# Two tiles' turns moved from TensorE to the DMA, and epsilon of two tiles moved to VectorE

## The chip, the core and the metric

The kernel runs on one core of one Trainium2 chip. The metric is the device time of one execution in microseconds (us). The kernel before takes 200.3 us, the median of three runs (200.17 to 200.72).

## What is computed

A parallel block: an attention branch A and a gated MLP branch B read the same normalised input, and both results are added to it.

```python
def _A_ref(x, wqkv, wo):            # 32 heads of 16; 8 keys, 2 apart, behind each query
    qkv = (x @ wqkv) ...
    logits = jnp.einsum('bhsd,bhswd->bhsw', q, kg) * scale
    attn = _softmax(where(mask, logits, -1e9))
    o = jnp.einsum('bhsw,bhswd->bhsd', attn, vg)
    return o.transpose(...) @ wo
def _B_ref(x, w_in, w_sp, b_sp, w_out):
    z = _gelu(x @ w_in)
    z1, z2 = z[..., :Fh], _layernorm(z[..., Fh:])
    g = jnp.einsum('ts,bsf->btf', w_sp, z2) + b_sp[None, :, None]
    return (z1 * g) @ w_out
xn = _layernorm(x)
return x + _A_ref(xn, A_wqkv, A_wo) + _B_ref(xn, B_w_in, B_w_sp, B_b_sp, B_w_out)
```

There are 2048 rows of x with 512 columns; Fh is 688. All inputs are bf16.

## The kernel before

The rows of x are 16 tiles of 128. Every step of the work is a named operation (`op_`, line 153) with a list of the operations it needs. Five lists at the end (lines 594 to 640), one for each of TensorE (`pe`), ScalarE (`act`), VectorE (`dve`), GpSimd (`pool`) and the SP queue (`sp`), fix by hand the order in which each engine runs its operations. So the order of an engine never changes at run time: an operation that waits holds up all that stand behind it in its list.

The names, in the order of the work (i is a tile):

- `x{i}` loads x, `b{i}` and `ag{i}` (lines 172 to 176) make mean and variance on VectorE, `gr{i}` (line 178) makes 1/sqrt(variance + epsilon) on GpSimd in two instructions, an add of epsilon (L179) and a power (L180), and `n{i}` normalises on VectorE (L183). Tile 0 is normalised in two halves, `n0a` and `n0` (L187).
- The normalised tile is turned, rows to columns, into `xnT`. Tiles 0 to 7 (`NPE = 8`) are turned by TensorE: `T{i}` (L216), four 128x128 blocks into PSUM, and `Tc{i}` (L219), a copy on ScalarE. Tiles 8 to 15 are turned by DMA from the SP queue: `t{i}` (L199).
- `z{i}` and `y{i}` (L234) are 8 matmuls each, the right and left half of x @ w_in. Their gelus are on ScalarE: `h{i}` (L251) and `yg{i}` (L314). The left half's result z1 lies over x and the normalised tiles in SBUF, so that y{i} may come only after certain norms.
- The right half z2 is normalised: statistics (`zt`, `sq`, `zs`), roots on GpSimd (`zr0`, `zr4`, `zr8`, `zr12`), the scaling on VectorE for tiles 0 to 7 and on ScalarE for 8 to 15 (`zn{i}`, L305).
- `k0`..`k7`, `q0`..`q7`, `v0`..`v7` (L325) are 32 matmuls each; ScalarE copies them out (`kc`, `qc`, `vc`, L338). `kh0a`, `kh0b`, `kh1` to `kh3` and `vh` (L343, L344) are small DMAs that copy halos of k and v between partitions.
- Products of q and k on VectorE, `m{c}{th}` (L363; the first is `m00`), folded by accumulating DMAs that GpSimd issues, `f{c}{th}` (L371), and summed into the logits, `p{c}{th}` (L376 to L379). Then the softmax of each half of the rows: `X`, `e`, `u`, `i`, `C`. `e` and `i` are on ScalarE (L420, L411 and L412), `u` (L406 to L408) on VectorE. `a0.*`, `a1.*` (L430, L434, L443) multiply with v and add. `HW` is a small memset on VectorE behind `p31`, which frees the third buffer of w_sp.
- `M0` to `M15` (L479) mix z2 with w_sp, 32 matmuls each; `W0` to `W7` load w_sp turned, each for two M. ScalarE empties M{j} as `G{j}` (L495), VectorE multiplies with z1, `g{j}` (L497), and SP turns the result, `U{j}` (L484).
- At the end both branches' output products are summed in PSUM (`gf`, `ao`: L533, L540, L544), x is added (`E`, `F`), and the rows are stored.

`psum("mm", ...)` (line 204) hands out three PSUM tiles in turn: a z, y, k, q, v or M may start only when the reader of the one three places ahead of it in the TensorE list is done. `psum("aux", ...)` has two tiles for the turns.

The lists around the change, as they are before:

```python
pe  = wu T0a T0 B wd z0a T1 z0b T2 z1 T3 z2 T4 z3 T5 z4 T6 z5 T7 z6 z7 y0 y1 z8 z9 ... z14  k0 k1 q0 q1 k2 k3 ...
sp  = x0 x1 x2 x3 x4 x5 x6 x8 wy x12 wk wq wv t8 t9 ... t15 W0 kh0a kh0b W1 kh1 vh W2 W3 LO0 LO1 W4 U0 ...
dve = b0 ag0 b1 ag1 n0a n0 b2 ag2 n1 b3 n2 ...  zn4 .. zn7 m00 f00 p00 m01 zs8 m10 ... p31 HW u0 X1 C0 g0 a0.0 u1 ...
act = ... EL e0 G0 i0 G1 e1 i1 G2 G3 ...
```

Of the kernel before, what the change touches and what calls it, by code (L numbers as in the profile page):

```python
# [10 lines left out]
ALU = mybir.AluOpType  # L11
# [5 lines left out]
NT = S // P  # L17
# [15 lines left out]
EPS = 1e-5  # L33
# [9 lines left out]
def kernel(  # L43
# [19 lines left out]
    x2 = A_x.rearrange("b s d -> (b s) d")  # L63
# [11 lines left out]
    mv = sb.tile([P, NT, 2], F32, name="mv")  # L75
    rstd = sb.tile([P, NT], F32, name="rstd")
# [33 lines left out]
    z2 = z2_r[:].rearrange("p (i f) -> p i f", i=NT)  # L110
# [42 lines left out]
    def op_(name, after, f):  # L153
        assert name not in do, name
        do[name], needs[name] = f, list(after)

    def tok(i):
        return f"Tc{i}" if i < NPE else f"t{i}"

    NPE = 8  # L160
    ALLX = [tok(i) for i in range(NT)]
    ALLN = [f"n{i}" for i in range(NT)]

# [8 lines left out]
    def bn(i):  # L172
        V.bn_stats(stats[:, i, :], xs[:, i, :])  # L173

    def ag(i):
        V.bn_aggr(mv[:, i, :], stats[:, i, :])

    def root(i, n):
        G.tensor_scalar(rstd[:, i:i + n], mv[:, i:i + n, 1], EPS, 1.0, ALU.add, ALU.mult)  # L179
        G.tensor_tensor(rstd[:, i:i + n], rstd[:, i:i + n], mhalf[:, 0:n], ALU.pow)  # L180

    def norm(eng, i):
        eng.tensor_scalar(xn[i % 8], xs[:, i, :], mv[:, i, 0:1], rstd[:, i:i + 1], ALU.subtract, ALU.mult)  # L183

    def norm_half(n):
        c = slice(n * D // 2, (n + 1) * D // 2)
        V.tensor_scalar(xn[0][:, c], xs[:, 0, c], mv[:, 0, 0:1], rstd[:, 0:1], ALU.subtract, ALU.mult)  # L187

    for i in range(NT):
        op_(f"b{i}", [f"x{LX[i]}"], lambda i=i: bn(i))  # L190
        op_(f"ag{i}", [f"b{i}"], lambda i=i: ag(i))
        op_(f"gr{i}", [f"ag{i}"], lambda i=i: root(i, 1))
        if i == 0:
            op_("n0a", ["gr0"], lambda: norm_half(0))
            op_("n0", ["n0a"], lambda: norm_half(1))
        else:
            op_(f"n{i}", [f"gr{i}"] + ([tok(i - 8)] if i >= 8 else []), lambda i=i: norm(V, i))
        if i >= NPE:
            op_(f"t{i}", [f"n{i}"], lambda i=i: SP.dma_start_transpose(xnT[:, :, i * P:(i + 1) * P], xn[i % 8]))  # L199
# [111 lines left out]
    def make_y(i):  # L311
        over = [f"n{j}" for j in range(i * FP // D, (i * FP + FH - 1) // D + 1)] if i < 8 else ALLN + ALLX
        t = psum("mm", f"y{i}", f"yg{i}", [tok(i)] + over + ["wy"], lambda t: z_part(t, i, 0))
        op_(f"yg{i}", [f"y{i}"], lambda: A.activation(  # L314
            z1u[:, i, 0:FH].rearrange("p (a b) -> p a b", a=2), t[:, :, 0:FHALF], ACT.Gelu_apprx_tanh))


# [63 lines left out]
    for c, th in BUF:  # L381
        n = f"{c}{th}"
# [147 lines left out]
    def gated_full(i, start, stop, c=slice(0, D)):  # L530
        th, t0 = i // 8, (i % 8) * P
        for m in range(MF):
            PE.matmul(po[i][:, c], uT[th][:, m, t0:t0 + P], wout[:, m, c], start=(start and m == 0), stop=(stop and m == MF - 1))  # L533

    def attention_out(n, start, stop):
        th, s = n // 2, n % 2
        for r in range(2):
            for g in range(4):
                p = slice(32 * g, 32 * g + RN[r])
                PE.matmul(po[groups[n][g]], rest[th][r][p, s * P:(s + 1) * P], wrest[r][p, :],  # L540
                          start=(start and r == 0), stop=False, tile_position=(32 * g, 0))
        for d in range(DH):
            for g in range(4):
                PE.matmul(po[groups[n][g]], op[32 * g:32 * g + 32, th, d, s * P:(s + 1) * P], wo_r[32 * g:32 * g + 32, d, :],  # L544
                          start=False, stop=(d == DH - 1 and (stop or groups[n][g] == groups[3][3])), tile_position=(32 * g, 0))

    U = [[f"U{j}" for j in range(8 * th, 8 * th + 8)] for th in range(2)]
    EVM = [f"G{j}" for j in range(NT)] + ["Bc", "Tc4"]
    for n in (0, 1):
        op_(f"gf{n}", LO + U[0] + EVM, lambda n=n: [gated_full(i, True, False) for i in groups[n]])  # L550
        op_(f"ao{n}", [f"gf{n}", "a0.11"] + [f"V0{g}" for g in range(4)], lambda n=n: attention_out(n, False, True))
# [37 lines left out]
    for n, (t, c) in enumerate(pieces):  # L589
# [1 line left out]
        op_(f"Sl{n}", [f"Fl{n}"], lambda n=n, c=c: (SP, A, SP)[n].dma_start(out2[il * P:(il + 1) * P, c], o_of(il)[:, c]))  # L591


    pe = """wu T0a T0 B wd z0a T1 z0b T2 z1 T3 z2 T4 z3 T5 z4 T6 z5 T7 z6 z7 y0 y1 z8 z9 z10 z11 z12 z13 z14
        k0 k1 q0 q1 k2 k3 q2 q3 k4 k5 q4 q5 k6 k7 q6 q7
        v0 v1 v2 v3 v4 v5 v6 v7 z15 y2 y3 y4 y5 y6 y7 y8 y9 y10 y11 y12 y13 y14 y15
        M0 M1 M2 M3 M4 M5 M6 M7 M8 M9 M10 M11 M12 M13 M14 M15
        gf0 gf1 ao0 ao1 gf2 ao2 ao3""".split() + [f"gf3.{i}" for i in tail] + ["gfl0", "gfl1", "gfl2"]
    for n in pe:
        a, x = n[0], n[1:]  # L600
        if n in do:
            continue
        if n == "T0a":
            make_T0()
        elif a == "T":
            make_T(int(x))
        elif n == "z0a":
            make_z0()
        elif a == "z":
            make_z(int(x))  # L610
        elif a == "y":
            make_y(int(x))
        elif a in "qkv":
            make_heads(a, int(x))
# [79 lines left out]
```

## Time and profile before

| | us |
|---|---|
| median of three runs | 200.3 |
| the profiled execution's own time | 200.27 |
| its span in the profile | 198.5 |
| TensorE busy in the span | 194.2 |
| VectorE busy | 178.4 |
| ScalarE busy | 89.4 |
| GpSimd busy | 49.3 |

The span leaves out 1.77 us of the execution's own time that lie around it. In the profile PE is TensorE, PEld its weight loads, DVE is VectorE, ACT is ScalarE, POOL is GpSimd; SP has no row of busy time, since it only issues DMAs, and SPq, ACTq rows are issues. L234 is line 234. A row of a timeline gives the start, the duration, the engine, the line, the operation, the tile that is written and those that are read, the count, and in brackets the idle time ahead of it with what ended it. In the chain the work that ended last is followed back; its rows give the start and the length of a piece. "DMA to landing" is the time from the issue until the data has arrived. Different source tiles have one name in some rows: z stands for z1 and z2 and what lies over them, qk for the two halves of q and k.

### The profile page before, as it was taken

The page shows a single profiled execution, that of the slowest core. Times are in us where ns is not written, and L with a number is a line of the kernel's source. Part 1 is how long each engine was busy: PE and PEld are TensorE (multiplying, and loading weights), DVE is VectorE, ACT ScalarE, POOL GpSimd, SP SyncE. Part 2 cuts the span into 40 slices and gives each one's busy share as a digit, 9 for nine tenths or more (in the row PEclk, how much of TensorE's full clock was granted, in tenths as well). Part 3 has the DMA queues.
Part 4 walks back from the last instruction along what each step waited for, and adds up shares of the span by engine and source line. Part 5 has one row for each costly group of instructions (what it writes and reads, how often), then busy time and mean ns, then how long its engine had stood idle before and what let it go on. Part 6 is the DMA issues. An engine that isn't in the chain of part 4 may idle for free.

```text
span 198.5 us, 4606 instructions
## 1 busy us (share of the span) xinstructions
PE 194.2 (98%) x1957; PEld 122.0 (61%) x1960; DVE 178.4 (90%) x205; ACT 89.4 (45%) x130; POOL 49.3 (25%) x83
## 2 busy tenths in 40 slices
PE   8999999999999999999999999999999999999993
PEld 2566666666666666666666666666666654444442
DVE  4899896999979999988999999999999999997244
ACT  2587797875559885991462311111222110044000
POOL 5567222005992249363000000010111000000000
PEclk9999999999999999999999999999999999999999
DMA  5999566860979999998299999999999969204233
GB/s 156 355 363 212 102 135 137 96 131 6 182 141 173 204 168 179 169 181 162 48 229 229 165 220 236 193 181 225 262 185 109 242 116 259 45 3 147 68 106 106
DMA packets 69076, 32.87 MB, mean 166 GB/s; under 512 B 57312, under 2 KB 67072, under 8 KB 68928
## 3 DMA queue, kind: packets, MB, share of 16 engines
q1 hardware_dynamic: 65680, 24.15, 58.2%
q0 software_dynamic: 2688, 7.70, 21.2%
q10 hardware_dynamic: 688, 0.74, 1.3%
q8 instruction: 15, 0.25, 0.5%
q14 instruction: 5, 0.04, 0.1%
HBM read 10.13 MB, written 2.10 MB: 62 GB/s over the span
## 4 chain that ended last, share of the span: by engine, by line
PE 94%; DMA 2%; DVE 1%; issue 1%; POOL 0%; SPq 0%; DVEq 0%
PE mm L479 38%; PE mm L325 21%; PE mm L234 18%; PE mm L544 7%; PE mm L533 6%; PE aux L533 2%; DMA z<-in_A_x_dram 2%; PE mm L540 1%; PE aux L216 1%; SPq L166 0%; DVE stats L173 0%; DVE z L590 0%; POOL rstd L180 0%; DVE z L183 0%; POOL rstd L179 0%
## 5 line engine op out<-in xcount | busy, mean ns | idle before, releaser
L479 PE MATMUL mm<-z,wsp 128*128 128x344 bf16 x512 | 74.8, 309 | 0.0
L479 PEld LDWEIGHTS <-wsp 128*128 128x128 bf16 x512 | 50.1, 98 | 24.6
L325 PE MATMUL mm<-xnT,wts 128*32 128x512 bf16 x768 | 41.7, 379 | 0.0
L234 PE MATMUL mm<-wts,xnT 128*128 128x344 bf16 x256 | 38.8, 309 | 0.0
L325 PEld LDWEIGHTS <-wts 128*32 128x32 bf16 x768 | 28.5, 138 | 13.0 <-issue 0.3
L430 DVE TENSOR_TENSOR prod<-vp,a_sb 128x4096 bf16<-128x4096 bf16 x16 | 36.2, 2283 | 0.0
L495 ACT ACTIVATE qk<-mm,b_col 128x688 bf16<-128x688 f32 x16 | 13.2, 830 | 42.8 <-PE mm L479 41.3
L234 PEld LDWEIGHTS <-xnT 128*128 128x128 bf16 x256 | 24.7, 98 | 11.8 <-issue 0.4
L363 DVE TENSOR_TENSOR prod<-qk 128x4096 bf16<-128x4096 bf16 x12 | 26.9, 2287 | 0.3 <-ACT qk L338 0.2
L434 DVE TENSOR_TENSOR prod<-prod,prod 128x8192 bf16<-128x8192 bf16 x6 | 26.5, 4420 | 0.1
L338 ACT CAST qk<-mm 128x1024 bf16<-128x1024 f32 x16 | 16.2, 1012 | 8.2 <-PE mm L325 8.2
L490 POOL DMA_DIRECT2D qk<-qk x8 | 3.9, 496 | 54.2 <-DMA qk<-z 49.6
L544 PE MATMUL mm<-wts,xnT 32*128 32x512 bf16 x192 | 14.5, 374 | 0.0
L314 ACT ACTIVATE z<-mm 128x688 bf16<-128x688 f32 x16 | 11.6, 744 | 3.4 <-PE mm L234 3.0
L533 PEld LDWEIGHTS <-qk 128*128 128x128 bf16 x75 | 7.2, 98 | 9.1 <-issue 0.8
L251 ACT ACTIVATE z<-mm 128x688 bf16<-128x688 f32 x16 | 11.9, 745 | 1.8 <-PE mm L234 1.8
L533 PE MATMUL mm<-wts,qk 128*128 128x512 bf16 x52 | 12.2, 379 | 0.3 <-issue 0.2
L173 DVE BATCH_NORM_STATS2 stats<-z 128x6 f32<-128x512 bf16 x16 | 10.7, 671 | 1.7 <-DMA z<-in_A_x_dram 1.7
L371 POOL DMA_DIRECT2D prod<-prod x10 | 9.4, 1132 | 8.4 <-DVE prod L363 8.4
L544 PEld LDWEIGHTS <-xnT 32*128 32x128 bf16 x256 | 6.5, 93 | 7.3
L578 ACT CAST z<-mm 128x512 bf16<-128x512 f32 x6 | 3.3, 600 | 13.7 <-PE mm L544 13.7
L338 ACT CAST vp<-mm 128x1024 bf16<-128x1024 f32 x8 | 8.1, 1011 | 2.7 <-PE mm L325 2.7
(92 smaller groups left out, 186.9 us busy)
## 6 DMA issues: line engine op xcount, KB each, us to landing
prod<-prod POOLq DMA_DIRECT2D x10, 512.0 KB, 8.5
wts<-in_A_wo_dram SPq DMA_DIRECT2D x4, 512.0 KB, 6.7
wsp<-in_A_x_dram SPq DMA_DIRECT2D x2, 1024.0 KB, 6.1
out_dram<-z SPq DMA_DIRECT2D x15, 128.0 KB, 1.8
wts<-in_A_wqkv_dram SPq DMA_DIRECT2D x3, 512.0 KB, 8.8
z<-in_A_x_dram SPq DMA_DIRECT2D x2, 512.0 KB, 6.4
wsp<-z POOLq DMA_DIRECT2D x2, 512.0 KB, 7.1
wsp<-wts POOLq DMA_DIRECT2D x2, 512.0 KB, 9.4
```

The costliest lines, as they stand in the source:

```text
L234: PE.matmul(t[:, hh, 0:FHALF], xnT[:, kc, i * P:(i + 1) * P], w_z[part][:, kc, hh * FHALF:(hh + 1) * FHALF], start=(kc == 0), stop=(kc == ...
L251: A.activation(z2[:, i, :].rearrange("p (a b) -> p a b", a=2), t[:, :, 0:FHALF], ACT.Gelu_apprx_tanh, **total)
L314: op_(f"yg{i}", [f"y{i}"], lambda: A.activation(z1u[:, i, 0:FH].rearrange("p (a b) -> p a b", a=2), t[:, :, 0:FHALF], ACT.Gelu_apprx_tanh))
L325: PE.matmul(t[32 * g:32 * g + 32, dd, :], w, r, start=(kc == 0), stop=(kc == C - 1), tile_position=(0, 32 * g))
L338: op_(f"{a}c{p}", [f"{a}{p}"], lambda: A.copy(home(a, p), t[:].rearrange("p d (t s) -> p d t s", t=2)))
L363: V.tensor_tensor(pr, q, k, ALU.mult)
L430: return lambda: V.tensor_tensor(dst, vp[:, :, th, off:off + GS], a_sb[:, th, W - 1 - w].unsqueeze(1).broadcast_to([P, DH, GS]), ALU.mult)
L434: return lambda: V.tensor_tensor(dst, dst, x, ALU.add)
L479: PE.matmul(t[:, hh, 0:FHALF], w[:, k, (j % 2) * P:(j % 2 + 1) * P], z2[:, k, hh * FHALF:(hh + 1) * FHALF], start=(k == 0), stop=(k == NT ...
L495: lambda: A.activation(gs[j % 3].rearrange("p (a b) -> p a b", a=2), t[:, :, 0:FHALF], ACT.Identity, bias=b_col[:, j:j + 1]))
L533: PE.matmul(po[i][:, c], uT[th][:, m, t0:t0 + P], wout[:, m, c], start=(start and m == 0), stop=(stop and m == MF - 1))
L544: PE.matmul(po[groups[n][g]], op[32 * g:32 * g + 32, th, d, s * P:(s + 1) * P], wo_r[32 * g:32 * g + 32, d, :], start=False, stop=(d == DH ...
```

## The change

Tiles 6 and 7 are turned by DMA: `NPE` is 6, `T6`, `T7` and their copies `Tc6`, `Tc7` go, and `t6`, `t7` come in the SP list. The TensorE list puts y0, y1 and y2 ahead of z6 and y3 ahead of z9 (before, y0 and y1 stood ahead of z8, and y2 and y3 after z15), and the gelus on ScalarE follow. On SP, wq goes behind t15, W0 behind kh0b, and wv and W1 behind kh1. The gelus of the y parts 10 to 15 name `p10` as a need, since in the new ScalarE list yg10 and yg11 stand ahead of zn12. Epsilon of tiles 0 and 1 is added by an instruction of VectorE, `ep0`, `ep1`, and GpSimd keeps the power alone for them; `ag1` and `ep1` stand behind the first half norm `n0a`.

```diff
-    NPE = 8
+    NPE = 6
...
     def root(i, n):
-        G.tensor_scalar(rstd[:, i:i + n], mv[:, i:i + n, 1], EPS, 1.0, ALU.add, ALU.mult)
+        if i not in (0, 1):
+            G.tensor_scalar(rstd[:, i:i + n], mv[:, i:i + n, 1], EPS, 1.0, ALU.add, ALU.mult)
         G.tensor_tensor(rstd[:, i:i + n], rstd[:, i:i + n], mhalf[:, 0:n], ALU.pow)
...
-        op_(f"gr{i}", [f"ag{i}"], lambda i=i: root(i, 1))
+        if i < 2:
+            op_(f"ep{i}", [f"ag{i}"], lambda i=i: V.tensor_scalar(rstd[:, i:i + 1], mv[:, i, 1:2], EPS, None, ALU.add))
+        op_(f"gr{i}", [f"ep{i}" if i < 2 else f"ag{i}"], lambda i=i: root(i, 1))
...
-        op_(f"yg{i}", [f"y{i}"], lambda: A.activation(
+        op_(f"yg{i}", [f"y{i}"] + ["p10"] * (i >= 10), lambda: A.activation(
...
-    EVM = [f"G{j}" for j in range(NT)] + ["Bc", "Tc4"]
+    EVM = [f"G{j}" for j in range(NT)] + ["Bc", "Tc5"]
...
-    pe = """wu T0a T0 B wd z0a T1 z0b T2 z1 T3 z2 T4 z3 T5 z4 T6 z5 T7 z6 z7 y0 y1 z8 z9 z10 z11 z12 z13 z14
+    pe = """wu T0a T0 B wd z0a T1 z0b T2 z1 T3 z2 T4 z3 T5 z4 z5 y0 y1 y2 z6 z7 z8 y3 z9 z10 z11 z12 z13 z14
         k0 k1 q0 q1 k2 k3 q2 q3 k4 k5 q4 q5 k6 k7 q6 q7
-        v0 v1 v2 v3 v4 v5 v6 v7 z15 y2 y3 y4 y5 y6 y7 y8 y9 y10 y11 y12 y13 y14 y15
+        v0 v1 v2 v3 v4 v5 v6 v7 z15 y4 y5 y6 y7 y8 y9 y10 y11 y12 y13 y14 y15
...
-    act = """wz0 wz1 GL Tc0a Tc0 Bc Tc1 Tc2 h0 Tc3 h1 Tc4 h2 Tc5 h3 Tc6 h4 Tc7 h5 h6 h7 yg0 yg1 h8 h9 sq8 h10 h11 sq9 h12 h13 h14 sq10
+    act = """wz0 wz1 GL Tc0a Tc0 Bc Tc1 Tc2 h0 Tc3 h1 Tc4 h2 Tc5 h3 h4 h5 yg0 yg1 yg2 h6 h7 h8 sq8 yg3 h9 h10 h11 sq9 h12 h13 h14 sq10
...
-        yg2 yg3 yg4 yg5 yg6 yg7 yg8 yg9 zn12 yg10 zn13 yg11 zn14 yg12 zn15 yg13 yg14 yg15 EL
+        yg4 yg5 yg6 yg7 yg8 yg9 yg10 yg11 zn12 yg12 zn13 yg13 zn14 yg14 zn15 yg15 EL
...
-    dve = """b0 ag0 b1 ag1 n0a n0 b2 ag2 n1 b3 n2 ag3 b4 ag4 n3 b5 ag5 n4 b6 ag6 b7 n5""".split()
+    dve = """b0 ag0 ep0 b1 n0a ag1 ep1 n0 b2 ag2 n1 b3 n2 ag3 b4 ag4 n3 b5 ag5 n4 b6 ag6 b7 n5""".split()
...
-    sp = """x0 x1 x2 x3 x4 x5 x6 x8 wy x12 wk wq wv t8 t9 t10 t11 t12 t13 t14 t15 W0 kh0a kh0b W1 kh1 vh
+    sp = """x0 x1 x2 x3 x4 x5 x6 x8 wy x12 wk t6 t7 t8 t9 t10 t11 t12 t13 t14 t15 wq kh0a kh0b W0 kh1 wv W1 vh
```

## The prediction

> **What bounds the kernel now.** I read the page's header and busy shares first, then the chain of work that ended last, then the timelines of VectorE and ScalarE (where each stretch begins and what ended the wait before it), then the DMA rows.
>
> ```profile
> span 198.5 us, 4606 instructions
> PE 194.2 (98%) x1957; PEld 122.0 (61%) x1960; DVE 178.4 (90%) x205; ACT 89.4 (45%) x130; POOL 49.3 (25%) x83
> PE 94%; DMA 2%; DVE 1%; issue 1%; POOL 0%; SPq 0%; DVEq 0%
> ```
>
> TensorE is busy 98% of the span and holds 94% of the chain. So an edit can help only by taking work off TensorE or by shortening its start, and it hurts if it makes TensorE wait once. VectorE, at 90%, is the second engine to watch: it has little room to make up lost time. The chain in order of time gives the stages:
>
> ```profile
> 8.05 0.40 PE aux L216 x4
> ...
> 13.89 0.22 PE aux L216 x4
> 14.11 1.17 PE mm L234 x8
> 15.28 0.22 PE aux L216 x4
> 15.50 12.83 PE mm L234 x88
> 28.34 41.60 PE mm L325 x768
> 69.94 17.61 PE mm L234 x120
> 87.54 74.67 PE mm L479 x512
> ...
> 183.70 3.46 PE mm L544 x64
> ```
>
> The two L216 rows are T6 and T7, 0.22 us each. One z or y part (8 matmuls) is 12.83/11 = 1.167 us. L325 is the 24 head groups, 1.733 us each. L479 is M0 to M15, 4.667 us each. Between 8.05 and 162 TensorE never waits.
>
> How close are the others? M_j writes one of three PSUM tiles, so it must wait until ScalarE's G_(j-3) has emptied it. ScalarE's list there is e0 G0 i0 G1 e1 i1 G2, and i1 waits for VectorE's u1:
>
> ```profile
> 107.99 0.42 ACT L411 ACTIVATE stmp<-stmp 128x256 f32<-128x256 f32 x1 [4.24 <-DVE stmp L408]
> 108.76 1.54 ACT L495 ACTIVATE qk<-mm,b_col 128x688 bf16<-128x688 f32 x2
> L495 ACT ACTIVATE qk<-mm,b_col 128x688 bf16<-128x688 f32 x16 | 13.2, 830 | 42.8 <-PE mm L479 41.3
> ```
>
> L408 is the last step of u1; ScalarE has waited 4.24 us for it, and i1 starts at 107.99. The L495 row of two is G2 and G3; one takes 0.83, so G2 ends at 109.59. M5 starts at 87.54 + 5 x 4.667 = 110.88. M5's PSUM tile is free only 1.29 us before it is wanted, about 1.24 after a handover of 0.05 (the n2 norm below ends at 7.99, its turn starts at 8.05). **This is the narrow place.** M6 needs G3, the second of that row, which comes 0.7 later while M6 comes 4.67 later than M5.
>
> **The change part by part.**
>
> *T6 and T7 leave TensorE.* From 13.89 on, TensorE runs z5 y0 y1 y2 z6 z7 z8 y3 z9 to z14: 14 parts, 14 x 1.167 = 16.33, so k0 starts at 30.22, 1.88 later than now (two more y ahead of it, two turns fewer). The heads end at 71.82; then z15 and y4 to y15, 13 parts, 13/15 of 17.61 = 15.26, and M0 starts at 87.08 instead of 87.54. Gain on TensorE: **0.46 us**.
>
> *The DMA turns t6, t7 and what they move.*
>
> ```profile
> 12.85 0.40 DVE L183 TENSOR_SCALAR z<-z,mv,rstd 128x512 bf16<-128x512 bf16 x1
> 8.93 1.82 SPq L245 DMA_DIRECT2D wts<-in_A_wqkv_dram  x1
> 15.24 11.09 SPq L199 DMA_TRANSPOSE xnT<-z  x8
> DMA to landing us min/median/max: 2.4/2.5/4.2
> wts<-in_A_wqkv_dram SPq DMA_DIRECT2D x3, 512.0 KB, 8.8
> wts<-in_B_w_out_dram SPq DMA_DIRECT2D x1, 640.0 KB, 4.9
> ```
>
> The first row is n6, done at 13.25; SP is idle since 10.75, and earlier without wq and wv. So t6 issues at 13.27 and, at 11.09/8 = 1.39 each, t7 at 14.66 and t15 at 25.8. With 2.4 to 4.2 to land: t6 at 15.7 to 17.5 (z6's turn is 18.56), t7 at 17.1 to 18.9 (z7's is 19.73), t15 at 28.2 to 30.0 (k0's is 30.22). None is late; the cover is the three y parts put ahead of z6. ScalarE loses two copies and its gelus follow TensorE one for one. A rule that speaks against the edit: the Trainium skill (VectorE: DVE Perf Modes, The three transpose paths) gives 1309 ns for one 128x128 block by DMA and 390 ns by TensorE. By that, a tile of four blocks would be an estimated 5.2 us, and t15 would land near 66, some 35 us after k0's turn; the trace disagrees, with four blocks every 1.39 us by DMA and in 0.22 us on TensorE.
>
> wq now follows t15, at about 27.0. It is wanted by q0 at 30.22 + 3.47 = 33.69. Its bounds are 4.9 and 8.8 to land, so 31.9 or 35.8. I take 4.9: that load also had only transposes beside it, while the 8.8 was queued in the opening burst of loads. At 8.8 q0 would wait 2.1.
>
> *W0, wv and W1 on SP.* Now kh1 waits behind W1, then wv and W1 behind kh1, which itself waits for kc3 of the heads.
>
> ```profile
> 34.95 5.33 SPq L456 DMA_TRANSPOSE wsp<-in_B_w_sp_dram  x1
> ...
> 41.03 0.65 SPq L344 DMA_DIRECT2D qk<-qk  x1
> ```
>
> kh1's second half leaves SP at 41.68, later by 1.88: 43.56. W0, now between kh0b and kh1, fills the slot that W1 has today. Then wv takes up to 1.82, as in its row, to 45.4, and W1 lands 6.2 later (W2's row below) near 51.6. v0 wants wv at 30.22 + 16 x 1.733 = 57.9; M0 and M2 want W0 and W1 at 87 and 96: hidden.
>
> *VectorE gets later.* This is the cost. Its product stretch starts when ScalarE has copied q0:
>
> ```profile
> 33.73 1.01 ACT L338 CAST qk<-mm 128x1024 bf16<-128x1024 f32 x1 [0.71 <-PE mm L325]
> 34.81 4.49 DVE L363 TENSOR_TENSOR prod<-qk 128x4096 bf16<-128x4096 bf16 x2 [0.24 <-ACT qk L338]
> 57.90 1.23 DVE L376 TENSOR_TENSOR a_sb<-prod 128x2048 bf16<-128x2048 bf16 x1 [1.21 <-DMA prod<-prod]
> 64.02 1.23 DVE L378 TENSOR_TENSOR wsp<-wsp 128x2048 bf16<-128x2048 bf16 x1 [0.31 <-DMA wsp<-z]
> 88.41 1.23 DVE L378 TENSOR_TENSOR prod<-prod 128x2048 bf16<-128x2048 bf16 x1 [0.68 <-DMA prod<-prod]
> 94.34 1.23 DVE L378 TENSOR_TENSOR prod<-prod 128x2048 bf16<-128x2048 bf16 x1 [0.43 <-DMA wts<-in_B_w_out_dram]
> 48.55 1.86 POOL L371 DMA_DIRECT2D prod<-prod  x2
> ```
>
> q0's copy ends at 34.74 and m00 starts at 34.81. k0 is 1.88 later, so q0, its copy and m00 are too (36.69). From there to u1 the VectorE list is unchanged and waits only in these four rows, 2.63 us, each for a fold by accumulating DMA. The folds come from POOL behind kh2 (which needs kc5 of the same head groups) and behind VectorE's own products, so they move by the same 1.88. Bounds for the lag at u1: 0, if all four waits shrink, and 3.1, if wv and W1 (to 51.6) cost the fold issued at 48.55 + 1.88 = 50.4 the 1.2 us that they overlap. I take **1.88**, by the row that sets m00.
>
> *Result at M5.* G2 ends at 109.59 + 1.88 = 111.47, M5 may start at 111.52; its turn is 87.08 + 23.33 = 110.41. TensorE waits **1.1 us**, and M5 starts 0.64 later than now. W2, which M4 wants at 87.08 + 18.67 = 105.75, is issued behind VectorE's memset HW:
>
> ```profile
> 96.86 9.25 SPq L456 DMA_TRANSPOSE wsp<-in_B_w_sp_dram  x2
> DMA to landing us min/median/max: 6.2/6.2/6.2
> 177.34 2.29 DVE L443 TENSOR_TENSOR xnT<-prod 128x4096 bf16<-128x4096 bf16 x1
> ```
>
> W2 would land at 96.86 + 1.88 + 6.2 = 104.94, 0.8 ahead. VectorE's last attention sum ends at 179.63 + 1.88 = 181.51; the matmuls that read it start at 183.70 + 0.64. Nothing else is late.
>
> *Epsilon on VectorE, tile 1's aggregate behind the first half norm.*
>
> ```profile
> 3.94 0.19 POOL L179 TENSOR_SCALAR rstd<-mv 128x1 f32<-128x1 f32 x1 [1.62 <-DVE mv L176]
> 4.21 0.58 POOL L180 TENSOR_TENSOR rstd<-rstd,mhalf 128x1 f32<-128x1 f32 x1
> 47.22 0.16 DVE L282 TENSOR_SCALAR zmean<-zsum 128x4 f32<-128x4 f32 x1
> 4.83 0.60 DVE L187 TENSOR_SCALAR z<-z,mv,rstd 128x256 bf16<-128x256 bf16 x2 [0.19 <-POOL rstd L180]
> 5.66 0.69 DVE L173 BATCH_NORM_STATS2 stats<-z 128x6 f32<-128x512 bf16 x1 [0.23 <-DMA z<-in_A_x_dram]
> 7.20 0.74 PE L234 MATMUL mm<-wts,xnT 128*128 128x344 bf16 x4
> 7.58 0.41 DVE L183 TENSOR_SCALAR z<-z,mv,rstd 128x512 bf16<-128x512 bf16 x1
> ```
>
> The add leaves POOL (0.27 from start to start) and costs VectorE about 0.19 with its handover (0.16 in the nearest row), so the first half norm starts 0.08 earlier. The second half waits behind tile 1's aggregate and add and ends near 5.64 instead of 5.43. That is when x2 lands (5.66), which sets b2, n2 (7.58) and the turn at 8.05. At most TensorE's 0.11 idle before 8.05 (7.94 to 8.05) can go, and 0.1 can come by b2. I take 0. What moves k0 here moves VectorE too.
>
> **Sum.** -0.46 + 1.10 + 0 = +0.64 on the profiled execution: span 199.1, time 200.27 + 0.64 = 200.91. The profiled time is 0.03 below the median of 200.3, so I forecast **200.9**. A difference under 0.3% (0.6 us) cannot be told from none here, and the forecast lies on that border.
>
> **Rivals.**
>
> *The lag is made up.* If the fold waits (2.63 us in all) shrink so that u1 is under 0.78 late (1.24 less the 0.46 gained), M5 never waits and only the turns count: 200.3 - 0.46 = 199.84, not slower. For it: the waits exist, and the early loads now lie elsewhere. Against it: each fold is issued behind work that is itself 1.88 late. From 0.78 on, every further 0.1 of lag takes 0.1 back.
>
> *More lag.* wv and W1 overlap the first fold, and p01 already waits 1.21 for it; each tenth that the fold loses goes straight to M5: up to 202.1. W1 may also end before the fold's packets begin, which speaks against it.
>
> *A DMA is late for TensorE.* wq at its upper bound stops q0 for 2.1, and VectorE lags by as much more: 200.9 + 2.1 = 203.0. Against it: what made 8.8 was the burst in front, which is over by then. If turns come 1.39 apart but every one takes the 4.2 to land, t15 still comes 0.2 ahead of k0. By the Trainium skill's 1309 ns a block (VectorE: DVE Perf Modes, The three transpose paths) k0 would be the one to wait, for an estimated 35 us; the rows of this trace leave no room for that.
>
> *The opening does more than I think.* All of the 0.11 idle before 8.05 gained moves M5 by no more than that: 200.8.
>
> **How the numbers follow.** Forecast, a wait at M5 of 0.5 to 1.6 with the opening's 0.1 either way: 0.67 (200.3 to 201.4; 0.35 above 200.9 and 0.32 below; the opening's rival is in it, at about 0.05). Lag made up: 0.18 (199.5 to 200.1; 0.08 of it below 199.7, if the opening gives too, and 0.10 above). More lag: 0.11 (201.4 to 202.1). DMA late: 0.04. The range 199.8 to 201.7 leaves out the lower edge of the second case, half of the third and the fourth. Faster 0.08; within 0.3% 0.32 + 0.10 = 0.42; slower 0.35 + 0.11 + 0.04 = 0.50.
>
> **What would show it.** Right: no L216 after the sixth tile's turn; the chain's first L325 at 30.2; the first L363 near 36.7, released by L338; the last L408 before G2 near 109.8; a gap of about 1.1 in TensorE near 110.4, released by L495; L479's row 1.1 longer than 74.67. Wrong: no gap there (the lag was made up); a gap before 30 or near 33.7 (a DMA); a wait at 57.9 + 1.88 longer than 1.21 (the fold).

## The result and the profile after

The changed kernel takes 201.64 us, the median of 13 runs (200.75 to 202.59). The kernel before takes 200.4 us in the same session (13 runs, 200.03 to 201.06). The ratio is 1.0062 with a 95% interval of 1.0048 to 1.0077: slower, by 1.24 us between the medians where 0.64 was forecast. Run again in a later session (e9 below) it took 201.38 us against 200.27: +1.11. The changed kernel's runs also lie further apart, 1.84 us from end to end against 1.03; what that is worth comes below.

The profiled execution took 202.2 us, 0.56 above its own median, with a span of 200.4 us against 198.5. Everything read from this profile belongs to one of the longer executions of the kernel; that matters below. From L194 on, a line of the changed kernel has a number three higher than before (L234 is L237, L325 is L328, L363 is L366, L408 is L411, L479 is L482, L495 is L498); so it is in e10, while e4 and e12 have the numbers of before.

From the page, after: the span, the busy shares, the engines' shares of the chain, then the row of the mixing matmuls (busy time, mean ns of one, idle time ahead of them and what ended most of it).

```profile
span 200.4 us, 4594 instructions
PE 193.8 (97%) x1949; PEld 121.2 (60%) x1952; DVE 178.6 (89%) x207; ACT 88.8 (44%) x128; POOL 49.0 (24%) x81
...
PE 63%; DVE 17%; DMA 10%; POOL 4%; issue 3%; ACT 1%; DVEq 0%; ACTq 0%
...
L482 PE MATMUL mm<-z,wsp 128*128 128x344 bf16 x512 | 75.1, 309 | 1.7 <-ACT qk L498 1.4
```

TensorE is busy 0.4 us less than before, which is the two turns. Yet the chain has gone from 94% TensorE to 63%: now it runs through VectorE and the folds by DMA. One row says why. The mixing matmuls, which never waited before, have 1.7 us of idle time, 1.4 of it ended by ScalarE's L498, the emptying of a PSUM tile.

The chain in order of time, after, shows where the path leaves TensorE and where it comes back:

```profile
12.74 17.50 PE mm L237 x120
30.24 17.46 PE mm L328 x320
47.72 1.02 ACT qk L341
...
88.20 8.71 DMA prod<-prod
97.01 1.24 DVE prod L381
...
111.52 0.73 ACT qk L498
112.29 51.49 PE mm L482 x352
```

From k0's start at 30.24 to 47.72 the path is TensorE's. Then it is the logits' path (copy, fold by DMA, sums, u1, i1, G2), and at 112.29 TensorE starts M5 because G2 has just ended. TensorE's timeline, after, shows the same from the other side (the brackets hold the idle time ahead of a row):

```profile
8.06 0.40 PE L219 MATMUL aux<-ident,z 128*128 128x128 bf16 x4
...
12.58 17.66 PE L237 MATMUL mm<-wts,xnT 128*128 128x344 bf16 x120
30.17 41.67 PE L328 MATMUL mm<-xnT,wts 128*32 128x512 bf16 x768
...
86.95 18.83 PE L482 MATMUL mm<-z,wsp 128*128 128x344 bf16 x128
106.05 4.83 PE L482 MATMUL mm<-z,wsp 128*128 128x344 bf16 x32 [0.27 <-DVE z L500]
112.29 51.49 PE L482 MATMUL mm<-z,wsp 128*128 128x344 bf16 x352 [1.42 <-ACT qk L498]
```

The bracket of 0.27 is M4's. It names g0 (L500), which M4 doesn't need. What M4 needed was W2, issued at 99.53 and landed 6.4 us later, at 105.9.

The kernel before has one row for all of M0 to M15:

```profile
87.38 74.83 PE L479 MATMUL mm<-z,wsp 128*128 128x344 bf16 x512
```

Up to M0 the change is a gain of 0.43 (86.95 against 87.38). At the end of M15 it is a loss: 163.78 (112.29 + 51.49) against 162.21 (87.38 + 74.83), so 1.57. Between them lie 2.00 us: the two brackets, 0.27 + 1.42, and 0.16 for each of the two restarts, since the profile gives a matmul 309 ns by itself, while in a stream each starts 146 ns (74.67 us / 512) behind the one ahead of it. Everything behind M15 keeps its distance as far as the last add. The rest of the 1.9 us between the spans, 0.33, lies behind that add. The prediction's sum has no term for it; it is explained under "The tail" below.

What follows here is the path to M5 on ScalarE and VectorE, after:

```profile
110.65 0.42 ACT L414 ACTIVATE stmp<-stmp 128x256 f32<-128x256 f32 x1 [4.24 <-DVE stmp L411]
...
111.42 1.54 ACT L498 ACTIVATE qk<-mm,b_col 128x688 bf16<-128x688 f32 x2
```

```profile
36.68 4.50 DVE L366 TENSOR_TENSOR prod<-qk 128x4096 bf16<-128x4096 bf16 x2 [2.08 <-ACT qk L341]
...
59.00 1.23 DVE L379 TENSOR_TENSOR a_sb<-prod 128x2048 bf16<-128x2048 bf16 x1 [0.44 <-DMA prod<-prod]
...
66.06 1.23 DVE L381 TENSOR_TENSOR wsp<-wsp 128x2048 bf16<-128x2048 bf16 x1 [1.25 <-DMA wsp<-z]
...
91.16 1.23 DVE L381 TENSOR_TENSOR prod<-prod 128x2048 bf16<-128x2048 bf16 x1 [1.39 <-DMA prod<-prod]
...
97.01 1.22 DVE L381 TENSOR_TENSOR prod<-prod 128x2048 bf16<-128x2048 bf16 x1 [0.35 <-DMA wts<-in_B_w_out_dram]
```

VectorE's first product starts at 36.68, 1.87 later than before, as forecast (36.69). From there to i1 nothing moves but the four waits for folds: 0.44 + 1.25 + 1.39 + 0.35 = 3.43 us where the profile of before had 2.63. (The last bracket names another load; the operation, p31, needs only its fold.) So i1 starts at 110.65, 2.66 later instead of 1.88, and M5 may start 1.64 after it, at 112.29.

Two sums can be taken from these rows and carried to every other profile below. First, i1 starts 70.5 us plus the fold waits after m00: before 107.99 - 34.81 - 2.63 = 70.55, after 110.65 - 36.68 - 3.43 = 70.54. Second, M5 starts at the later of TensorE's own turn, M0 + 23.33, and i1 + 1.64. Before, that is 110.71 against 109.63, a margin of 1.08; after, 110.28 against 112.29.

### The profile page after: what moved, and what is told of

It is laid out like the page before. It is cut to its first block, busy times and chain, and to the rows that moved or that the text cites. A ratio compares the mean times of both kernels' runs of the same rounds, so it can differ in the third digit from the quotient of the medians.

```text
span 200.4 us, 4594 instructions
## 1 busy us (share of the span) xinstructions
PE 193.8 (97%) x1949; PEld 121.2 (60%) x1952; DVE 178.6 (89%) x207; ACT 88.8 (44%) x128; POOL 49.0 (24%) x81
## 4 chain that ended last, share of the span: by engine, by line
PE 63%; DVE 17%; DMA 10%; POOL 4%; issue 3%; ACT 1%; DVEq 0%; ACTq 0%
PE mm L482 26%; PE mm L237 11%; PE mm L328 9%; PE mm L547 7%; PE mm L536 6%; DMA prod<-prod 4%; DVE prod L366 4%; DMA wsp<-z 4%; DVE a_sb L382 2%; PE aux L536 2%; DVE prod L381 2%; DVE stmp L409 1%; DMA z<-in_A_x_dram 1%; POOL prod L374 1%; POOL zrstd L292 1%
## 5 line engine op out<-in xcount | busy, mean ns | idle before, releaser
L482 PE MATMUL mm<-z,wsp 128*128 128x344 bf16 x512 | 75.1, 309 | 1.7 <-ACT qk L498 1.4
L482 PEld LDWEIGHTS <-wsp 128*128 128x128 bf16 x512 | 50.0, 98 | 26.7 <-issue 1.6
L328 PE MATMUL mm<-xnT,wts 128*32 128x512 bf16 x768 | 41.7, 379 | 0.0
L237 PE MATMUL mm<-wts,xnT 128*128 128x344 bf16 x256 | 38.5, 309 | 0.0
L328 PEld LDWEIGHTS <-wts 128*32 128x32 bf16 x768 | 28.2, 139 | 13.3 <-issue 0.3
L237 PEld LDWEIGHTS <-xnT 128*128 128x128 bf16 x256 | 24.8, 98 | 12.1 <-issue 0.4
L498 ACT ACTIVATE qk<-mm,b_col 128x688 bf16<-128x688 f32 x16 | 13.2, 830 | 41.7 <-PE mm L482 40.2
L366 DVE TENSOR_TENSOR prod<-qk 128x4096 bf16<-128x4096 bf16 x12 | 26.9, 2287 | 2.2 <-ACT qk L341 2.1
L181 POOL TENSOR_TENSOR rstd<-rstd,mhalf 128x1 f32<-128x1 f32 x16 | 9.0, 563 | 3.8 <-DVE rstd L194 2.7
```

Source lines behind the costliest of these rows:

```text
L237: PE.matmul(t[:, hh, 0:FHALF], xnT[:, kc, i * P:(i + 1) * P], w_z[part][:, kc, hh * FHALF:(hh + 1) * FHALF], start=(kc == 0), stop=(kc == ...
L328: PE.matmul(t[32 * g:32 * g + 32, dd, :], w, r, start=(kc == 0), stop=(kc == C - 1), tile_position=(0, 32 * g))
L366: V.tensor_tensor(pr, q, k, ALU.mult)
L482: PE.matmul(t[:, hh, 0:FHALF], w[:, k, (j % 2) * P:(j % 2 + 1) * P], z2[:, k, hh * FHALF:(hh + 1) * FHALF], start=(k == 0), stop=(k == NT ...
L498: lambda: A.activation(gs[j % 3].rearrange("p (a b) -> p a b", a=2), t[:, :, 0:FHALF], ACT.Identity, bias=b_col[:, j:j + 1]))
```

## The experiments

Each was timed beside the kernel before on the same chip, and the difference to that kernel's median in the same session is given. e1 to e4 ran together (before 200.28), e5 to e8 (200.35), and e9 to e12 (200.27).

**e1: G2 ahead of i1, in the changed kernel.** If M5 waits because G2 stands behind i1 in ScalarE's fixed list, and for no other reason, the wait goes.

```diff
-        e0 G0 i0 G1 e1 i1 G2 G3
+        e0 G0 i0 G1 e1 G2 i1 G3
```

> The changed kernel with one edit to ScalarE's list: G2 stands ahead of i1 instead of behind it. Theory (VectorE's lag holds back i1, i1 holds back G2, G2 holds M5): the 1.4 us wait of TensorE at M5 goes, G2 ends near 107.3; what stays is the wait of M4 for W2 (0 to 0.3) and the gain of two turns, so 200.2 (199.8 to 200.4) against 201.6 of the change and 200.4 of the kernel before. Rival (TensorE loses its time elsewhere: the opening, the DMA turns, a slower last stage): the time stays within 0.3 of the change, about 201.5.

Measured: 200.14 us (199.93 to 200.8), -0.14; ratio 0.999, 95% interval 0.9967 to 1.0014. ScalarE and TensorE in its profile:

```profile
105.14 0.81 ACT L498 ACTIVATE qk<-mm,b_col 128x688 bf16<-128x688 f32 x1
...
109.47 0.42 ACT L414 ACTIVATE stmp<-stmp 128x256 f32<-128x256 f32 x1 [3.51 <-DVE stmp L411]
```

```profile
87.05 74.83 PE L482 MATMUL mm<-z,wsp 128*128 128x344 bf16 x512
```

G2 is done at 105.95, before ScalarE begins to wait for u1. i1 is still later than in the kernel before (109.47 against 107.99), but TensorE no longer cares: 512 matmuls in one piece of 74.83. The loss at M5 is gone. So that loss is the order of two entries in ScalarE's list together with a later u1; it isn't the late u1 by itself.

**e2: the same edit in the kernel before.** This tells whether e1 repairs the change or would have helped anyway.

```diff
-        e0 G0 i0 G1 e1 i1 G2 G3 ...
+        e0 G0 i0 G1 e1 G2 i1 G3 ...
```

> The kernel before with the same edit, G2 ahead of i1. Theory: before, M5 does not wait, so the edit gives nothing, 200.4 (200.1 to 200.6), with a smaller spread at most. Rival (G2's place costs something of its own in either kernel): a gain of about 1 us as in the changed one.

Measured: 200.21 us (200.02 to 202.22), -0.07; ratio 1.0, interval 0.9967 to 1.0034. Without the change there is no wait at M5 to remove. Its runs lie 2.2 us apart, so the edit didn't make them closer together either.

**e3: the kernel before with y2 and y3 ahead of k0.** Their gelus on ScalarE follow, and those from 10 on name `p10` as a need, as in the change. No turn goes to the DMA, and SP's list and the opening stay.

```diff
-    ... T6 z5 T7 z6 z7 y0 y1 z8 z9 z10 ...
+    ... T6 z5 T7 z6 z7 y0 y1 y2 z8 y3 z9 z10 ...
...
-        v0 v1 v2 v3 v4 v5 v6 v7 z15 y2 y3 y4 ...
+        v0 v1 v2 v3 v4 v5 v6 v7 z15 y4 ...
```

> The kernel before with only the TensorE and ScalarE order of the y parts changed: y2 and y3 ahead of k0, all eight turns on TensorE, the loads and the opening as before. Theory: k0 and the products of VectorE start 2.33 later, TensorE gains nothing, so M5 waits 2.33 - 1.24 = 1.1 or up to 0.8 more if the folds come later again as in the changed kernel: 201.5 to 202.3. Rival (what delays VectorE are the moved loads wq, wv, W0, W1 or the DMA turns): no wait, 200.4.

Measured: 201.34 us (200.56 to 202.15), +1.06; ratio 1.0043, interval 1.0017 to 1.0069. Its VectorE, ScalarE and TensorE rows:

```profile
36.95 4.49 DVE L363 TENSOR_TENSOR prod<-qk 128x4096 bf16<-128x4096 bf16 x2 [2.53 <-ACT qk L338]
```

```profile
109.67 0.42 ACT L411 ACTIVATE stmp<-stmp 128x256 f32<-128x256 f32 x1 [4.24 <-DVE stmp L408]
```

```profile
87.22 23.50 PE L479 MATMUL mm<-z,wsp 128*128 128x344 bf16 x160
111.31 51.49 PE L479 MATMUL mm<-z,wsp 128*128 128x344 bf16 x352 [0.59 <-ACT qk L495]
```

Two y parts ahead of k0 make the same wait at the same place, released by the same emptying. i1 + 1.64 is 111.31 here too. So the reorder of TensorE's list is enough to do the harm, without the DMA turns and SP's new order. The time is a little below the expected 201.5 to 202.3, which counted on later folds: m00 comes 2.14 later than before, and less the margin of 1.08 that is the +1.06 measured.

**e5: the changed kernel with y2 and y3 back behind z15.** The gelus follow. The DMA turns stay, and their cover shrinks to y0 and y1.

```diff
-    ... z5 y0 y1 y2 z6 z7 z8 y3 z9 z10 ...
+    ... z5 y0 y1 z6 z7 z8 z9 z10 ...
...
-        v0 v1 v2 v3 v4 v5 v6 v7 z15 y4 ...
+        v0 v1 v2 v3 v4 v5 v6 v7 z15 y2 y3 y4 ...
```

> The changed kernel with y2 and y3 behind z15 again, as before; the DMA turns, the loads and the opening stay changed. Theory (the y parts ahead of k0 make VectorE late, but they are also what hides the turns): k0's turn comes at 27.9, but t15 issues at 26.2 and lands near 28.7 and wq near 33, so TensorE waits near 28 for 0.5 to 1.0 and perhaps up to 1 more at q0; VectorE's lag at u1 falls under 1.3, the wait at M5 goes: 200.3 to 201.3. Rival (the lag comes from the moved loads or the turns, not from the y parts): the first product still starts near 36.7 and M5 still waits over 1 us: 201.5 or more.

Measured: 200.85 us (200.45 to 201.74), +0.50; ratio 1.003, interval 1.0017 to 1.0044. TensorE in its profile:

```profile
12.62 15.62 PE L237 MATMUL mm<-wts,xnT 128*128 128x344 bf16 x104
28.17 41.67 PE L328 MATMUL mm<-xnT,wts 128*32 128x512 bf16 x768
...
87.28 74.83 PE L482 MATMUL mm<-z,wsp 128*128 128x344 bf16 x512
```

The first row holds 13 parts, 13 x 1.167 = 15.17, and lasts until k0 starts 15.55 later, 0.38 more. In the changed kernel it holds 15 parts, 17.50, and k0 starts after 17.59, 0.09 more. So TensorE loses some 0.3 here, in gaps too small for the view to show. That the turns cause them is likely but not shown. If they do, the two y parts bought a cover of 0.3, less than the 0.5 to 1.0 expected. No wait is left at M5: i1 is at 108.03 and M5 could start at 109.67, 0.94 ahead of its turn at 110.61. By its profile (200.53 us) this version loses what the turns gave to k0's delay and to the tail, which comes next; its median is 0.3 above that profile, and what its longer executions lose stays open.

**e7: two more DMAs in the kernel before.** The changed kernel issues two DMAs more than the one before (t6 and t7), and its span ends 2.98 us after the last add where it was 2.66. Here wv is loaded in three pieces instead of one, so that the count of DMAs rises by two and all else stays as before.

```diff
-    op_("wv", [], lambda: SP.dma_start(w_v, wq_d[:, :, 2 * D:3 * D]))
+    op_("wv", [], lambda: [SP.dma_start(w_v[:, a:b], wq_d[:, a:b, 2 * D:3 * D]) for a, b in ((0, 2), (2, 3), (3, 4))])
```

> The kernel before with wv loaded in three DMAs instead of one, two more in all, nothing else. Theory of the tail: the last store's semaphore becomes the second of the closing series, the time behind VectorE's last add grows from 2.66 to 3.0, 200.3 becomes 200.6. Rival: 2.66 stays and the time too. A wait at the heads or the folds is not expected from it, since v0 wants wv only at 57.

Measured: 200.83 us (200.41 to 202.49), +0.48; ratio 1.0024, interval 1.0006 to 1.0043. The span and VectorE's last add:

```profile
span 198.6 us, 4608 instructions
```

```profile
195.33 0.28 DVE L590 TENSOR_TENSOR z<-aux,stmp 128x128 bf16<-128x128 f32 x1
```

The work ends at 195.61, 0.23 earlier than in the profile of before, and the span is 0.1 longer: 2.99 us behind the last add, with two DMAs more, far from the end.

**e11: the changed kernel with six DMAs more.** wq and wv are loaded in four pieces each, so there are eight DMAs more than before.

```diff
-    op_("wq", [], lambda: SP.dma_start(w_q, wq_d[:, :, 0:D]))
-    op_("wv", [], lambda: SP.dma_start(w_v, wq_d[:, :, 2 * D:3 * D]))
+    op_("wq", [], lambda: [SP.dma_start(w_q[:, a:b], wq_d[:, a:b, 0:D]) for a, b in ((0, 1), (1, 2), (2, 3), (3, 4))])
+    op_("wv", [], lambda: [SP.dma_start(w_v[:, a:b], wq_d[:, a:b, 2 * D:3 * D]) for a, b in ((0, 1), (1, 2), (2, 3), (3, 4))])
```

> The changed kernel with wq and wv loaded in four DMAs each, six DMAs more, so that the last store's semaphore stands last again among the closing waits. Theory: the tail is 2.65 instead of 3.0, the wait ahead of M5 stays near 1.4, time 0.3 below the changed kernel of the same call (201.3 if that is 201.6). Rival, the smaller loads also make VectorE earlier: the wait ahead of M5 goes below 0.7 and the time falls by 1.0.

Measured: 200.9 us (200.24 to 202.04), +0.63; ratio 1.0021, interval 0.9997 to 1.0045, which just takes in no change. Against the changed kernel timed beside it (e9) it is 0.48 faster. The span is 198.4 and the last add ends at 195.8: 2.6 us, the short tail again, with six DMAs *more*. TensorE and the fold waits of the profiled execution (200.24 us, the shortest of its runs):

```profile
110.67 51.49 PE L482 MATMUL mm<-z,wsp 128*128 128x344 bf16 x352 [0.36 <-ACT qk L498]
```

```profile
36.54 4.49 DVE L366 TENSOR_TENSOR prod<-qk 128x4096 bf16<-128x4096 bf16 x2 [2.08 <-ACT qk L341]
...
59.34 1.23 DVE L379 TENSOR_TENSOR a_sb<-prod 128x2048 bf16<-128x2048 bf16 x1 [0.92 <-DMA prod<-prod]
...
65.42 1.22 DVE L381 TENSOR_TENSOR wsp<-wsp 128x2048 bf16<-128x2048 bf16 x1 [0.27 <-DMA wsp<-z]
...
89.43 1.23 DVE L381 TENSOR_TENSOR prod<-prod 128x2048 bf16<-128x2048 bf16 x1 [0.21 <-DMA prod<-prod]
...
95.39 1.23 DVE L381 TENSOR_TENSOR prod<-prod 128x2048 bf16<-128x2048 bf16 x1 [0.45 <-DMA prod<-prod]
```

The wait ahead of M5 is 0.36, not the 1.4 expected. Here the folds cost 1.85 us instead of 3.43, m00 starts at 36.54, and 36.54 + 70.5 + 1.85 is 108.9, with i1 at 109.03 in this profile. The rival in the expectation, that the smaller loads make VectorE earlier, can't be told apart by this one execution from the scatter of the folds; the median fell by 0.48, far less than its 1.0.

**e6: G2 ahead of i1 and the six more DMAs, in the changed kernel.** Both costs are taken away together.

```diff
-    op_("wq", [], lambda: SP.dma_start(w_q, wq_d[:, :, 0:D]))
+    op_("wq", [], lambda: [SP.dma_start(w_q[:, a:b], wq_d[:, a:b, 0:D]) for a, b in ((0, 1), (1, 2), (2, 3), (3, 4))])
...
-        e0 G0 i0 G1 e1 i1 G2 G3 ...
+        e0 G0 i0 G1 e1 G2 i1 G3 ...
```

wv is loaded as wq is.

> The changed kernel with G2 ahead of i1 and with wq and wv loaded in four DMAs each instead of one, six more DMAs in all. Theory of the tail (the closing waits of SP are passed one after another in a fixed order of eight semaphores, about 0.06 us each; two more DMAs have moved the last store from the last of them to the second): with six more the last store has the last one again, the time behind VectorE's last add falls from 2.99 to 2.65, so 0.3 less than with G2 alone: 199.8 (199.6 to 200.1). Rival (the longer tail comes from the output stores that start later): the tail stays at 3.0 and the time at 200.1.

Measured: 199.86 us (199.68 to 200.5), -0.49; ratio 0.9977, interval 0.9966 to 0.9988. This beats both kernels. The last add ends at 195.72 and the span at 198.4 (2.7), and M0 to M15 run without a gap:

```profile
87.25 74.83 PE L482 MATMUL mm<-z,wsp 128*128 128x344 bf16 x512
...
195.44 0.28 DVE L593 TENSOR_TENSOR z<-aux,stmp 128x128 bf16<-128x128 f32 x1
```

With the wait and the longer tail gone, the median leaves what was forecast for the two turns, -0.46. The profiled execution (200.14) is above that median and doesn't show the gain: its turn of tile 2 is at 8.36 instead of 8.05, behind a late load of x, and M0 is only 0.13 earlier than before.

**e9: the changed kernel again**, beside e10 to e12.

> The changed kernel as it is, on the same chip as the next three. If the parts add up as the earlier runs say: 201.6 (200.9 to 202.0), with a wait of about 1.4 ahead of M5 and 3.0 behind the last add. If the 0.4 between it and the run without the opening edits was only the other chip: 201.2, the same as there.

Measured: 201.38 us (200.76 to 202.71), +1.11; ratio 1.0052, interval 1.003 to 1.0074. Its profiled execution (202.0 us) has fold waits of 0.46, 1.18, 1.43 and 0.31, 3.38 in all, i1 at 110.47 and M5 at 112.11. The median lies between the two that were expected (201.6 and 201.2) and decides for neither.

**e4, e10 and e12: the opening.** e4 undoes the opening edits in the changed kernel, e12 undoes them in e6, and e10 puts them alone into the kernel before. The main lines of the edit of e4 and e12 (`ep0` and `ep1` go with them; e10 is its reverse):

```diff
-        if i not in (0, 1):
-            G.tensor_scalar(rstd[:, i:i + n], mv[:, i:i + n, 1], EPS, 1.0, ALU.add, ALU.mult)
+        G.tensor_scalar(rstd[:, i:i + n], mv[:, i:i + n, 1], EPS, 1.0, ALU.add, ALU.mult)
...
-    dve = """b0 ag0 ep0 b1 n0a ag1 ep1 n0 b2 ...
+    dve = """b0 ag0 b1 ag1 n0a n0 b2 ...
```

> The changed kernel with the opening as before: epsilon added by GpSimd for all tiles, tile 1's aggregate ahead of the first half norm. Theory (x2's load sets the opening): 201.6, within 0.2 of the change. Rival (the two adds on VectorE or the later second half norm delay TensorE's start): 0.2 to 0.5 faster than the change, or, if the opening gains, that much slower.

> The kernel before with the opening edits alone (epsilon of tiles 0 and 1 by VectorE, tile 1's aggregate behind the first half norm). Theory, x2's load sets the opening: same as before within 0.15, tile 2's turn at 8.05 as before. Rival, the opening edits cost (or gain) by themselves: 0.3 or more slower (or faster), with tile 2's turn, and so k0, that much later (or earlier).

> The best version so far (G2 ahead of i1, wq and wv in four DMAs each) with the opening edits undone, tile 1's epsilon on GpSimd again and its aggregate ahead of the first half norm. Theory, the opening edits are worth nothing: 199.86 as with them, within 0.15. Rival, they cost: 0.2 to 0.4 faster than with them, 199.5.

Measured: e4 201.22 us (200.47 to 202.5), +0.94; ratio 1.0044, interval 1.0013 to 1.0074. e10 200.39 us (200.16 to 200.97), +0.12; ratio 1.0001, interval 0.9983 to 1.0019. e12 199.96 us (199.62 to 200.46), -0.31; ratio 0.9975, interval 0.9956 to 0.9993, beside 0.9977 for e6. e4 alone settled nothing, since the changed kernel's runs lie 1.8 us apart. e10 and e12 have no wait at M5 in their profiles, and both say that the opening edits are worth nothing that can be measured. e10's turn of tile 2, and the wait ahead of it on VectorE:

```profile
7.04 0.69 DVE L173 BATCH_NORM_STATS2 stats<-z 128x6 f32<-128x512 bf16 x1 [0.32 <-DMA z<-in_A_x_dram]
```

```profile
8.10 0.40 PE L219 MATMUL aux<-ident,z 128*128 128x128 bf16 x4
```

It is at 8.10 against 8.05 before. A load of x sets it, though not always x2's: in this profile b2 doesn't wait, and the row is b3, which waits for x3 and stands ahead of n2 in VectorE's list.

**e8: e6, and HW three places earlier**, so that W2 would be loaded sooner (M4 waited 0.27 for it in the changed kernel's profile).

```diff
-    op_("HW", [f"p{c}{th}" for c, th in BUF], lambda: V.memset(wsp_r[2][0:1, 0:2], 0.0))
+    op_("HW", ["p10", "p21"], lambda: V.memset(wsp_r[2][0:1, 0:2], 0.0))
...
-        ... p21 p30 X0 p31 HW u0 ...
+        ... p21 HW p30 X0 p31 u0 ...
```

> As the run with G2 early and six more DMAs, and the memset HW behind p21, the last reader of its buffer, instead of behind p31, so that W2 is issued near 89 instead of 98 to 99. Theory (M4 waits for W2 by up to 0.3 when VectorE is late): that wait cannot come, 199.7 (199.5 to 200.0) with less spread. Rival (W2 earlier collides with the folds f30 and f31 on the DMA engines): VectorE's waits for them grow by about 1 us; as G2 no longer waits for u1 the time stays at 199.8, unless M3 or M4 comes to wait for G0 or G1, 200.5.

Measured: 200.7 us (199.75 to 201.77), +0.35; ratio 1.0016, interval 0.9995 to 1.0037. The expectation failed: it is 0.84 slower than e6. W2 was issued at 90.52 instead of 99.25, and one fold wait grew. SP, VectorE and TensorE in its profile:

```profile
90.52 17.41 SPq L459 DMA_TRANSPOSE wsp<-in_B_w_sp_dram  x2
```

```profile
6.34 0.69 DVE L173 BATCH_NORM_STATS2 stats<-z 128x6 f32<-128x512 bf16 x1 [0.66 <-DMA z<-in_A_x_dram]
...
98.07 1.23 DVE L381 TENSOR_TENSOR prod<-prod 128x2048 bf16<-128x2048 bf16 x1 [2.06 <-DMA prod<-prod]
```

```profile
87.63 75.00 PE L482 MATMUL mm<-z,wsp 128*128 128x344 bf16 x512
```

2.06 us for the last fold is longer than in any other profile of this study (0.31 to 0.77 where it shows), which fits W2's load running beside that fold. W2 itself took 15.8 us to land, where it took 6.2 in e6, and came at 106.3. That is M4's own turn (87.63 + 18.67) and later than e6's W2, at 105.4, so the earlier issue bought nothing. M0 to M15 lose 0.17 (75.00 against 74.83), at M4, where the weight loads stop until 106.44. By the end of M15 this profile is 0.55 behind that of e6, and the other 0.38 of it was lost in the opening: b2 waited 0.66 for x2's load, and tile 2's turn and k0 are 0.38 later. The two kernels are the same up to HW, so that part is scatter. What makes this version's median slow stays open.

## Where the difference went

Four kernels differ only in the place of G2 and in the count of DMAs (the six more come from wq and wv in pieces), each against the kernel before in its own session:

| | G2 behind i1 | G2 ahead of i1 |
|---|---|---|
| two DMAs more than before | +1.24, +1.11 (the change, e9) | -0.14 (e1) |
| eight DMAs more | +0.63 (e11) | -0.49 (e6) |

Read across: the wait at M5 costs 1.1 to 1.4. Read down: the tail, with whatever the loads in pieces do besides, costs 0.35 to 0.6 by medians; by the time behind the last add alone it costs 0.3 to 0.4. What remains in the last cell is the gain of the turns.

**The scatter of the folds.** The fold waits add up to 3.43, 3.38 (e9), 1.85 (e11), 2.16 (e1), 2.86 (e6), 2.86 (e12), 2.23 (e3) and 1.88 (e4) us in eight profiles with y2 and y3 ahead of k0, and to 2.63, 2.91 (e5), 3.23 (e7), 3.29 (e10) and 0.43 (e2) in the five without. In e2 VectorE also waited 0.81 for a halo copy ahead of m01, which may have left the folds more time. So these profiles don't say that the change made the folds slower. They scatter without any edit: e1 is the changed kernel up to the place of G2, behind the last of these waits, and so is e2 the kernel before. e1 has 2.16 where the changed kernel had 3.43, and e2 has 0.43 where the kernel before had 2.63. Before, M5's margin (1.08 in its profile; 0.21 in e10's, where i1 starts at 108.92) hid most of that. With u1 1.87 later the margin is spent, and each tenth that a fold loses makes M5 a tenth later.

That this is why the changed kernel's runs lie further apart (1.84 us against 1.03) is argued and not shown. The middle half of the runs spans 0.51 us against 0.48, and in the other sessions the kernel before had ends 1.14, 2.21 and 2.84 us apart.

**The tail.** Behind the last add come two stores, then closing waits on SP, and the program ends. The stores cost the same in both kernels:

```profile
195.57 0.88 SPq L591 DMA_DIRECT2D out_dram<-z  x2
```

```profile
197.15 0.88 SPq L594 DMA_DIRECT2D out_dram<-z  x2
```

The closing waits are listed in the view of the kernel's last line. Before, in the window from 196 to 197 and then from 197 to 197.6:

```profile
L689 SPq EVENT_SEMAPHORE  x6: 28/28/28, 196.5 to 196.9; - x6
...
L689 SPq EVENT_SEMAPHORE  x3: 27/28/28, 197.2 to 197.6; - x3
```

After, from 198.2 to 199 and then from 199 to 200 (the wait at 198.98 stands in both, and the one at 199.8 comes behind the closing waits):

```profile
L692 SPq EVENT_SEMAPHORE  x1: 28/28/28, 199.0 to 199.0; - x1
...
L692 SPq EVENT_SEMAPHORE  x9: 17/28/28, 199.0 to 199.8; - x9
```

Before, most of the waits pass while the last store is still under way, and the last store's wait is the last of them, at 197.58 in the trace. After, the last store's semaphore stands third in the row; it passes at 199.16, and six more waits, long since fulfilled, follow at 0.06 us each until 199.52. The waits go through eight semaphores of these DMAs in the order of their numbers, 102 to 109, in both kernels. In the trace the stores take these numbers one after another, and the last store has 109 before and 103 after. So two more DMAs move it to another place in a fixed row of waits. In both kernels its wait passes 1.5 us after it is issued, so the store itself isn't slower. The profiles with the count of before or eight more (before, e2, e3, e6, e8, e10, e11, e12) have 2.6 to 2.7 us behind the last add; those with two more (after, e1, e4, e5, e7, e9) have 2.96 to 3.05. That the count decides is shown by e7 and e11 in both directions; counts other than these weren't tried.

## The prediction, step by step

*The turns' gain* was right: M0 starts 0.43 earlier (forecast 0.46), and e6's median is 0.49 below the kernel before.

*The DMA turns, wq, W0, kh1, wv and W1 in time* was right. Ten turns take 14.23 us on SP, 1.42 each (forecast 1.39), and TensorE runs from 12.58 to the end of the heads without a gap; after, on SP:

```profile
13.30 14.23 SPq L202 DMA_TRANSPOSE xnT<-z  x10
27.58 0.58 SPq L247 DMA_DIRECT2D wts<-in_A_wqkv_dram  x1
```

So the rival "a DMA is late for TensorE" is out. The Trainium skill (VectorE: DVE Perf Modes, The three transpose paths) gives 1309 ns for one 128x128 block by DMA; the trace disagrees with the estimate of 5.2 us for a tile of four that was worked out from it, since a tile came every 1.42 us.

*k0 and VectorE's first product 1.88 later* was right: 30.24 (30.22) and 36.68 (36.69). *The opening at nothing* was right in size: tile 2's turn is at 8.06 (8.05 before), and e10 and e12 find no difference. The reason given, x2's load, holds in part: the turn waits for a load of x, but in e10 for x3's, through b3.

*The wait at M5 through u1, i1 and G2* was right in its place, its releaser and its cause, as e1 and e3 show from both sides. Two of its terms were off. The margin was taken as 1.24 and is 1.08: 110.88 was worked out from the chain, which counts a streaming matmul from the end of the one ahead, while a matmul that has waited is counted from its own start, as in the timeline, where M5's turn was 110.71. By the lag of 1.88 the forecast of +0.64 should have been +0.80. The lag at u1 was taken as 1.88; at i1, which follows it, it is 2.66 in the profiled execution, since the fold waits came to 3.43 instead of 2.63. The bound of 3.1 held it, but not for the reason given: the wait that wv and W1 were to lengthen, p01's, fell from 1.21 to 0.44. Over all profiles the folds lie on both sides of 2.63, so for the median 1.88 was a fair size, and the profile of after overstates it, as its 202.2 us overstate the kernel's time.

*W2 in time for M4* was off: forecast 0.8 ahead, M4 waits 0.27 for it in the profile, for it follows HW, which follows the same folds. It costs nothing here, since M5 waits for G2 until later anyway.

*The tail* is the step that was missing. The prediction let everything behind M15 move as one, and counted the two added DMAs only by their time on the queue. By the profiles they cost 0.33 at the end.

Together: 0.80 for M5 and 0.33 for the tail are +1.13, against medians of +1.24 and +1.11.

That 201.64 still lies in the range of 199.8 to 201.7, by 0.06, is luck in part. It is past the 200.3 to 201.4 that the prediction gave to its own case, in the stretch that it gave to "more lag" (201.4 to 202.1). But the rival's mechanism, a longer wait at p01, didn't come; what came instead, 0.16 from a margin taken too large and 0.33 from the tail, is 0.49 of the 0.60 between the forecast difference and the measured one.

## What to carry to other kernels

In a list of fixed order, work on the busiest engine that is moved ahead of a producer delays everything behind that producer; look for the place where an emptying of PSUM that is already possible stands behind an entry that waits for that chain, and swap the two before you judge the move. A margin of 1 us that is fed by DMAs that scatter by more than 1 us isn't a margin, and one profile can't size what is left of it. When a change alters the number of DMAs, compare the time between the last instruction and the end of the span before explaining a few tenths by anything else.

## What was not expected of the hardware

- Two DMAs more, far from the end of the program, turned the 2.65 us from the last add to the end into 3.0, and six more on top turned them back (e7, e11): closing waits that are long fulfilled still pass one after another, 0.06 us each.
- The waits for the folds, which are accumulating DMAs of 512 KB, scatter from one execution to the next: they came to 2.16 and 3.43 us in two kernels that are the same up to there (e1 and the changed kernel).
- The same transposing load of w_sp, W2, took 6.2 us to land when it was issued behind the folds (e6) and 15.8 us when it was issued beside the last one (e8).
- A stop in a stream of matmuls costs 0.16 us more than the idle time in its bracket, the difference between the 309 ns that the profile gives one matmul and the 146 ns between the starts of two.
